# A fused attention and MLP-mixer kernel: rounding steps behind squares, pools in another order, sums and transposes at other places, last stores split

## The chip, the cores and the metric

The kernel runs on one core of a Trainium2 chip. The metric is the device time of one execution in microseconds (us), the median of several runs. A core has a matrix engine (TensorE, PE in the profile), a vector engine (VectorE, DVE), a scalar engine (ScalarE, ACT), GpSimd (POOL), and SyncE (SP), which here only issues DMAs. Each engine runs its own list of instructions in order, and waits where it needs what another one makes.

## The reference

Attention without a softmax, normalised by row and head, and then an MLP mixer over tokens and over channels. With B = 8, H = 8 heads, S = 576 tokens, D = 64 (512 channels):

```python
kv = einsum('bhsd,bhse->bhde', k, v)
o = einsum('bhsd,bhde->bhse', q, kv)
x = o / sqrt(mean(o * o, -1) + 1e-6) * g_norm            # then to (B, S, 512)
h = maximum(x.T @ w_tok1, 0) @ w_tok2                    # 576 -> 256 -> 576, over tokens
u = x + h.T
out = u + maximum(u @ w_ch1, 0) @ w_ch2                  # 512 -> 1536 -> 512, over channels
```

q, k and v are 32-bit floats. The four weights are 64-bit floats, which the kernel rounds to 32 bits itself; all matmuls are in 32 bits.

## The kernel before

**Attention and token mixing** work on pairs of batch elements, four pairs. For each pair, `kv` steps make the products of k and v, `a0` to `a4` make the attention outputs (`a4` is the remainder of 64 tokens of both elements), and for each of them `q` (square, on ACT), `g` (times `g_norm`, on DVE), `t` (sum of squares, on DVE), `m`, `r` and `i` (mean, root, inverse) and `s`, `d` or `p` (scaling on ACT, DVE or POOL) follow. `h..` and `hr` are the first token matmul, `u0` to `u8` the second; `z` copies an x tile into PSUM ahead of `u` as its start (a seed). The attention outputs of `a` stand in two PSUM buffers (`ps_o`, or `ps_r` for the remainder), so the tile after `a4` starts when the squares and gains of `a4` have read theirs. u is stored to DRAM by POOL's queue, and read back later.

The x tiles of even pairs come from the pool `xp0`, of odd pairs from `xp1`. The pools on the left side of SBUF lie in the order in which they are made, and the pools of the next stage take their room from the bottom when they are closed: first the three sums of `w_ch1` that `mix_ch1` makes (`late["w2"]`, 18,432 bytes a partition, as much as `xp0`), then the transposed u of the rest unit, then working buffers.

**The order of the work** is written out by hand: `play` reads lists of names, `start`, `middle`, `steady[0]`, `steady[1]` and `last`, one after the other. `middle` does the attention of pair 1 beside the token mixing of pair 0, and so on. A digit in them takes that many steps from the stream of rounding: for each of 14 blocks of the channel weights `scale` (two ACT instructions of 768 or 1024 elements a partition, which wait for the raw weights), `clamp`, `shift` and `add` (DVE). The scaling of the next block comes in one step with the shift of the one before. `lq0` loads q (transposed, `qT`) for the next pair, `l..` loads k and v, `f..` the raw weights, `x..` transposes u in blocks; all these DMAs are issued by SP, in one queue. As `a4` ends the use of one of the two `qT` buffers, `lq0` stands behind it.

**The rest unit.** Channel mixing has nine units of 512 tokens: eight of one batch element each, and one of the eight remainders of 64. The rest unit goes first and alone (`channel1_once`, `channel2_once`).

**Channel mixing** of the other units goes in four stages `g` of two units each, 1 to 4. Both matmuls use a scheme of seven products in place of eight, twice nested: an outer product `o` of sums of blocks of u (`outer_u`) and of the weights, and in it seven inner products (`inner_u`, places by `PLACE`) in three PSUM names, `ps_a`, `ps_b` (one buffer each) and `ps_d` (two). `put` files steps under a place; a place is one inner product on PE, about 1.30 us, and the steps follow it. `channel1` begins at place `b`; its outer product number i starts at `b + 7i`, and reads `ps_a` out at `b + 7i + 4` in its `second` (with a base, by a DVE addition, else by an ACT copy). The matmul at `b + 7i + 7` writes `ps_a` again. `add(3, 3, 1)` adds v1 to v3 in two halves, `turn_blocks` transposes u for the next stage from `xt`, four times with the DVE for each unit, and `put_blocks` stores every second result; `fetch_t` loads `xt`, of which there are two buffers.

**The end.** In the last outer product of the last stage the results go onto `xg` (u, read back), together with the sums of other outer products (`xadd`). `store_part` stores two of the four row tiles of the last batch element, `store_rest` the columns 256 to 511 of all remainders.

## Time and profile before

| | us |
|---|---|
| median of 3 runs | 805.42 (805.23 to 805.69) |
| the profiled execution, its own time | 807.61 |
| its span, first to last instruction | 805.80 |
| PE busy | 778.9 (97%) |
| DVE busy | 613.1 (76%) |
| ACT busy | 265.8 (33%) |
| POOL busy | 78.3 (10%) |
| mean DMA rate | 237 GB/s over the span |

Stages by the profile: attention and token mixing to about 203 us, the rest unit to 275.6, and then four stages of some 131 us. The profile has, for each instruction, when it started and how long it took, and for idle time ahead of it which engine or DMA ended that; in a timeline the columns are the start and the duration in us, the engine (with q: its queue, which issues), the line, the operation, its tiles, and in brackets the idle time before it. A table of waits has the total, the number and the longest. For stages it has the busy time of each engine and, last in the row, the clock granted to PE (1.00 is full), the busy share of the DMA engines and GB/s. PE's idle time matters most, since PE is busy nearly throughout; the issue of a DMA and its landing are apart by the time in the queue.

### The profile page before, as it was taken

The page shows a single profiled execution, that of the slowest core. Times are in us where ns is not written, and L with a number is a line of the kernel's source. Part 1 is how long each engine was busy: PE and PEld are TensorE (multiplying, and loading weights), DVE is VectorE, ACT ScalarE, POOL GpSimd, SP SyncE. Part 2 cuts the span into 40 slices and gives each one's busy share as a digit, 9 for nine tenths or more (in the row PEclk, how much of TensorE's full clock was granted, in tenths as well). Part 3 has the DMA queues.
Part 4 walks back from the last instruction along what each step waited for, and adds up shares of the span by engine and source line. Part 5 has one row for each costly group of instructions (what it writes and reads, how often), then busy time and mean ns, then how long its engine had stood idle before and what let it go on. Part 6 is the DMA issues. An engine that isn't in the chain of part 4 may idle for free.

```text
span 805.8 us, 14820 instructions
## 1 busy us (share of the span) xinstructions
PE 778.9 (97%) x5832; PEld 654.2 (81%) x5832; DVE 613.1 (76%) x906; ACT 265.8 (33%) x513; POOL 78.3 (10%) x91
## 2 busy tenths in 40 slices
PE   6999989999999999999999999999999999999996
PEld 5655545543888888899988899998889998889996
DVE  2667867679666877988867889877798875788975
ACT  2356454655120123521133251122352113325210
POOL 1211111021530000001100001010000110000101
PEclk9999989999999999999999999999999999999999
DMA  9999999676689795598997579889559889555864
GB/s 294 311 344 328 364 309 381 227 267 227 222 285 318 274 334 166 155 282 215 252 235 222 156 207 272 249 195 285 141 154 298 200 230 231 169 156 145 206 151 79
DMA packets 128117, 192.11 MB, mean 238 GB/s; under 512 B 9392, under 2 KB 87728, under 8 KB 128048
## 3 DMA queue, kind: packets, MB, share of 16 engines
q1 hardware_dynamic: 111760, 167.67, 66.2%
q0 software_dynamic: 14656, 22.02, 13.4%
q10 hardware_dynamic: 1632, 1.47, 0.6%
q8 instruction: 46, 0.75, 0.4%
q14 instruction: 23, 0.19, 0.1%
HBM read 138.31 MB, written 52.82 MB: 237 GB/s over the span
## 4 chain that ended last, share of the span: by engine, by line
PE 73%; DVE 2%; issue 1%; ACT 0%; DVEq 0%
PE ps_d L132 27%; PE ps_a L132 18%; PE ps_b L132 18%; PE ps_v L132 5%; PE ps_c L132 3%; PE ps_w L132 2%; PE ps_u L132 1%; DVE us L123 1%; DVE v L123 0%; DVE u L123 0%; DVE ui L123 0%; DVE w_ch L173 0%; DVE w_ch L168 0%; ACT ps_u L129 0%; DVE xg L123 0%
## 5 line engine op out<-in xcount | busy, mean ns | idle before, releaser
L132 PE MATMUL ps_d<-ui,w 128*128 128x256 f32 x504 | 118.6, 379 | 0.0
L132 PEld LDWEIGHTS ps_d<-ui,w 128*128 128x128 f32 x504 | 95.2, 190 | 12.7
L123 DVE TENSOR_TENSOR v<-v,v 128x1536 f32<-128x1536 f32 (+2 forms) x70 | 103.5, 1484 | 0.3
L129 ACT COPY ps_d<-ps_a 128x768 f32<-128x768 f32 (+1 forms) x56 | 32.0, 571 | 210.2 <-PE ps_a L132 210.2
L132 PE MATMUL ps_b<-w,sv 128*128 128x128 f32 x672 | 84.6, 276 | 0.0
L132 PE MATMUL ps_a<-w,v 128*128 128x128 f32 x672 | 84.2, 275 | 0.0
L132 PEld LDWEIGHTS ps_a<-w,v 128*128 128x128 f32 x672 | 79.9, 192 | 0.2
L132 PEld LDWEIGHTS ps_b<-w,sv 128*128 128x128 f32 x672 | 79.5, 192 | 0.2
L132 PE MATMUL ps_u<-h,w_tok 128*128 128x512 f32 (+1 forms) x160 | 69.5, 621 | 1.8 <-ACT ps_u L129 1.5
L132 PE MATMUL ps_d<-w,v 128*128 128x128 f32 x528 | 66.2, 275 | 0.0
L132 PE MATMUL ps_h<-x,w_tok 128*128 128x512 f32 (+1 forms) x160 | 65.5, 603 | 0.1
L126 ACT ACTIVATE v<-v 128x768 f32<-128x768 f32 (+1 forms) x54 | 42.6, 821 | 66.2 <-DVE v L123 60.6
L132 PEld LDWEIGHTS ps_d<-w,v 128*128 128x128 f32 x528 | 62.7, 192 | 0.2
L132 PE MATMUL ps_d<-w,sv 128*128 128x128 f32 x480 | 60.1, 275 | 0.0
L132 PEld LDWEIGHTS ps_d<-w,sv 128*128 128x128 f32 x480 | 57.1, 192 | 0.2
L132 PEld LDWEIGHTS ps_u<-h,w_tok 128*128 128x128 f32 (+1 forms) x160 | 25.5, 184 | 34.2 <-issue 26.7
L132 PEld LDWEIGHTS ps_h<-x,w_tok 128*128 128x128 f32 (+1 forms) x160 | 26.1, 189 | 32.1 <-issue 28.2
L132 PE MATMUL ps_a<-uT,w 128*128 128x256 f32 x192 | 47.1, 381 | 4.9 <-DVE v L123 4.9
L1116 POOL DMA_DIRECT2D out_dram<-us x11 | 14.1, 1278 | 386.7 <-ACT us L129 345.6
L132 PEld LDWEIGHTS ps_a<-uT,w 128*128 128x128 f32 x192 | 35.9, 190 | 11.1 <-DVE v L123 6.5
L439 DVE TENSOR_TENSOR x<-ps_o,g_sb 128x512 f32<-128x512 f32 x32 | 21.5, 687 | 29.9 <-PE ps_o L132 25.1
L123 DVE TENSOR_TENSOR v<-ps_b,u 128x768 f32<-128x768 f32 x28 | 26.7, 954 | 22.5 <-PE ps_b L132 22.0
(145 smaller groups left out, 1233.4 us busy)
## 6 DMA issues: line engine op xcount, KB each, us to landing
w<-parts SPq DMA_DIRECT2D x168, 384.0 KB, 3.9
w<-parts SPq DMA_DIRECT2D x56, 192.0 KB, 3.3
qT<-in_q_dram SPq DMA_DIRECT2D x8, 1152.0 KB, 9.9
uT<-blocks SPq DMA_DIRECT2D x36, 256.0 KB, 5.5
k_in<-in_k_dram SPq DMA_DIRECT2D x16, 512.0 KB, 9.0
out_dram<-x POOLq DMA_DIRECT2D x16, 512.0 KB, 5.9
v_in<-in_v_dram SPq DMA_DIRECT2D x14, 512.0 KB, 9.7
raw<-in_moe_w_ch_dram SPq DMA_DIRECT2D x8, 768.0 KB, 9.6
```

Source lines behind the costliest of these rows:

```text
L123: keep(engine.tensor_tensor(out=o, in0=a, in1=b, op=op))
L126: keep(nc.scalar.activation(o, a, AF.Relu))
L129: keep(nc.scalar.copy(o, a))
L132: keep(nc.tensor.matmul(*a, **kw))
L439: keep(nc.vector.tensor_mul(x, bank[c, h], g_sb.to_broadcast([P, number(c), D])))
L1116: keep(nc.gpsimd.dma_start(to.rearrange("t p e -> p t e"), a, accum_op=ALU.add))
```

## The change

- `xp0` is made after `inp` (k, v, g), `qtp` (q) and `work`, so that it lies above them.
- In `middle` a rounding step moves from the row of `u5` to the end of the row of `a4`; in `steady[0]` one moves from the row of `u4` to the same place. Both are steps with a scaling.
- In `channel1` the two halves of `add(3, 3, 1)` move from places 17 and 22 to 21 and 24, the first four `turn_blocks` (with their `put_blocks` and `fetch_t`) from 5, 8, 11 and 14 to 3, 6, 9 and 12, and the fourth subtraction of `outer_u` from 17 to 25.
- At the end the second half's `xadd` of product 5 moves from 47 to 44 and the first half's from 45 to 46. `store_rest` moves from 48 to 45. The last element's second half is stored in two pieces: columns 384 to 511 from ACT's queue at 48, and columns 256 to 383 from SP's at 49.

```diff
-    xps = [pool("xp0", 4, "left", left), pool("xp1", 4, "right", right)]
+    xp1 = pool("xp1", 4, "right", right)
     inp = pool("inp", 1, "left", left)
     qtp = pool("qtp", 2, "left", left)
     work = pool("work", 1, "left", left)
+    xps = [pool("xp0", 4, "left", left), xp1]
...
-        for place, step in zip((17, 22), add(3, 3, 1)):
+        for place, step in zip((21, 24), add(3, 3, 1)):
...
-        for k, place in enumerate((5, 8, 11, 14, 50, 52, 67, 77)):
+        for k, place in enumerate((3, 6, 9, 12, 50, 52, 67, 77)):
...
-        for place, step in zip((-2, 1, -1, 17), outer_u(g)):
+        for place, step in zip((-2, 1, -1, 25), outer_u(g)):
...
-            for place, steps in ((38, [xadd(0, 6)]), (41, [xadd(1, 7)]), (45, [xadd(0, 5)]),
-                                 (47, [xadd(1, 5)]),
-                                 (48, [do(store_part, 0, 2), do(store_rest)]), (49, [do(store_part, 2, 4)])):
+            for place, steps in ((38, [xadd(0, 6)]), (41, [xadd(1, 7)]), (44, [xadd(1, 5)]),
+                                 (45, [store_rest]), (46, [xadd(0, 5)]),
+                                 (48, [do(store_part, nc.scalar, 2, 4, P, DH), do(store_part, nc.sync, 0, 2, 0, DH)]),
+                                 (49, [do(store_part, nc.sync, 2, 4, 0, P)])):
...
-    def store_part(lo, hi):
-        dma(out[B - 1, lo * P:hi * P, DH:].rearrange("(t p) e -> p t e", p=P), xg[NG - 1][:, lo:hi])
+    def store_part(queue, lo, hi, a, z):
+        dma(out[B - 1, lo * P:hi * P, DH + a:DH + z].rearrange("(t p) e -> p t e", p=P),
+            xg[NG - 1][:, lo:hi, a:z], queue)
...
-        "u4 z6 f1", "a2 q20 g21 q21 g20 s10", "u5 t20 t21 1 f2", "a4 q40 g41 q41 g40 lq0", "u6 t40 t41 1 l10",
+        "u4 z6 f1", "a2 q20 g21 q21 g20 s10", "u5 t20 t21 f2", "a4 q40 g41 q41 g40 lq0 1", "u6 t40 t41 1 l10",
...
-        "u4 z6 1 l11", "a4 q40 g41 q41 g40 lq0", "u5 d11 t40 t41 1", "a3 q30 g31 q31 g30 lq1",
+        "u4 z6 l11", "a4 q40 g41 q41 g40 lq0 1", "u5 d11 t40 t41 1", "a3 q30 g31 q31 g30 lq1",
```

## The prediction

> **What bounds the kernel now.** First the page's head and the table of who waited for whom, TensorE alone.

> ```profile
> span 805.8 us, 14820 instructions
> PE 778.9 (97%) x5832; PEld 654.2 (81%) x5832; DVE 613.1 (76%) x906; ACT 265.8 (33%) x513; POOL 78.3 (10%) x91
> PE ps_kv L132 <- DMA v_in<-in_v_dram: 7.1, 2, 6.4
> PE ps_a L132 <- DVE v L123: 4.9, 4, 1.2
> PE ps_o L132 <- ACT sq L443: 4.9, 3, 3.3
> PE ps_u L132 <- ACT ps_u L129: 1.5, 1, 1.5
> ```

> TensorE is the bound: it is idle 26.9 us, of which 6.4 are the first load and 7.2 come after its last matmul. No change to busy DVE or ACT time pays as such; only a removed wait of PE, or a shorter end, does. So each wait was looked up in the timelines. The largest:

> ```profile
> 111.60 1.98 PE L132 MATMUL ps_u<-h,w_tok 128*128 128x512 f32 x4
> 116.89 2.17 PE L132 MATMUL ps_o<-kvp,qT 64*64 64x64 f32 x64 [3.31 <-ACT sq L443]
> 114.64 0.89 ACT L158 ACTIVATE w_ch<-raw 128x768 f32<-128x768 f32 x1 [1.77 <-DMA raw<-in_moe_w_ch_dram]
> 116.19 0.65 ACT L443 ACTIVATE sq<-ps_r 128x256 f32<-128x256 f32 x2
> 118.00:120.00 2.00, 2.00 (x40) 1.37 (x36) 2.00 (x5) 0.60 (x1) 0.72 (x1) 0.50 1.13 374
> ```

> The remainder tile `a4` ended at 111.7, but its squares started at 116.19: ahead of them on ACT stood a scaling of rounding that waited for its weights until 114.64. The next attention tile needs the same PSUM buffers, so PE stood 3.31 us, and then ran at half clock (the last line is a stage: its third number from the end is the granted clock, 0.50). From the start of that tile to the next `ps_kv` took 126.41 - 116.89 = 9.52 us; the same instructions a pair later took 169.32 - 162.55 = 6.77. The slow clock thus cost 2.75 us more. The like wait in `middle` (72.42) is 1.03 us with no loss of clock.

> The other three places:

> ```profile
> 182.23 1.76 DVE L123 TENSOR_TENSOR w<-w_ch 128x1536 f32<-128x1536 f32 x1 [5.10 <-DMA out_dram<-x]
> 191.09 1.17 ACT L158 ACTIVATE w_ch<-raw 128x1024 f32<-128x1024 f32 x1 [3.25 <-DVE w_ch L173]
> 193.84 9.00 PE L132 MATMUL ps_u<-h,w_tok 128*128 128x512 f32 x24 [1.53 <-ACT ps_u L129]
> 429.66 1.75 DVE L123 TENSOR_TENSOR v<-v,v 128x1536 f32<-128x1536 f32 x1
> 431.33 1.22 DVE L123 TENSOR_TENSOR us<-uT,us 128x1024 f32<-128x1024 f32 x1
> 432.46 0.95 DVE L123 TENSOR_TENSOR v<-ps_a,v 128x768 f32<-128x768 f32 x1
> 433.47 1.56 PE L132 MATMUL ps_a<-uT,w 128*128 128x256 f32 x6 [1.23 <-DVE v L123]
> 798.48 2.45 SPq L120 DMA_DIRECT2D out_dram<-xg  x3
> 798.68 0.42 DVE L123 TENSOR_TENSOR xg<-ps_d,xg 128x256 f32<-128x256 f32 x1 [0.23 <-PE ps_d L132]
> ```

> At 182 the sums of `w_ch1` wait for stores out of the x tiles whose room they take; DVE, then ACT's scaling, then a seed copy, then PE are late in turn. At 429 a 1.75 us sum and a 1.22 us subtraction stand ahead of the read of `ps_a` that PE's place 21 needs. At the end three stores queue on SP.

> [...] half clock came 2.7 us into the 3.31 us wait and stayed 6.8 us; the 1.53 us wait did nothing. [...] those engines are over 95% busy from 104 to 140 us.

> **Part 1, scalings behind the squares** (rows `a4` of `middle` and `steady[0]`). No instruction is added. The squares then run at 111.8 to 112.5, after the seed copy `z6`, and the a3 tile follows `u5` at once. At its face this is worth 1.03 + 3.31 + 2.75 = 7.1 us. What is late next: the scaling still waits to 114.6, ends at 116.3, and the a3 squares and DVE's `add` of the rounding stand behind it (DVE to about 117). So a3's statistics come only 3.35 us earlier than 124.9. They feed `x` tiles that PE needs only after `a0` of the next pair, so they are hidden. But that `a0` needs a transfer:

> ```profile
> qT<-in_q_dram SPq DMA_DIRECT2D x1, 1152.0 KB, 10.3
> 135.91 1.16 PE L132 MATMUL ps_o<-kvp,qT 64*64 64x64 f32 x64
> ```

> It is issued at 121.04 and lands at 131.3 (10.3 later) in a full queue; `a0` came at 135.91, so 4.6 us of slack stood behind it. PE would now come at 135.91 - 7.1 = 128.8 (the steps one by one, with 0.1 for a3's buffers: 129.0). Nor can qT come earlier: its issue is held by the queue, not by a buffer, with at most 0.5 us of idle DMA (100 to 108, shares 0.92 and 0.96) to use. Rather later: the stores of this pair's last u tiles (issued 126.75 to 130.04; 1.05 MB, 2.6 us of all DMA engines by the per-queue shares) move up by some 3.4 us and interleave ahead of it. Before, 0.3 us of them lay ahead of 131.3. Bounds for the landing: 130.8 (only the idle DMA time used) to 133.6 (all stores ahead). I take 132.5. PE then waits 3.5 us and resumes 3.4 us earlier than before. Such a wait (3.31) halved the clock before[...]. I take yes, two chances in three, at the same 2.75. Part 1 nets -3.4 + 2.75 = **-0.65 us** (-3.4 with full clock).

> **Part 2, even x tiles above the inputs.** The sums now take the room of k, v and g, last read at 149.7 (kv) and 166.5 (gains), in place of that of tiles stored until 181.9. DVE starts them at 177.1 and all behind moves 5.1 us forward: rounding's add ends about 186, ACT's scaling goes straight after the seed copies (187.8), the seed is in place before 192.3. **-1.53 us**. Where the stall goes: nowhere near; later work of `last` is PE's own. If the sums waited elsewhere, the cost is the 1.53 kept.

> **Part 3, channel mixing, places 3 to 25** (four stages). The sum's halves go from 17 and 22 to 21 and 24, the subtraction from 17 to 25. DVE reads `ps_a` at 429.75 in place of 432.46, done before PE's place 21 at 432.25. -1.23 each. What is late next: the sum (1.75) at 24 and the subtraction (1.22) at 25 end at 441.3, so the read of `ps_b` at 26 ends at 442.2, and PE writes `ps_b` at 442.6: 0.4 us left. The transposes (0.7 us each) at 3, 6, 9, 12 fit DVE's idle 1.95 us before 412.93 and the gap before 418.04. Each brings its DMAs along SP's queue: four of blocks, one fetch of xt. They pass one 384 KB weight fetch, which lands about 3 us later than 421.47; it is used at 429.5: hidden. In the first stage xt is late: the fourth transpose waited until 295.46 for a transfer of 7.0 us. Now it stands before a read of `ps_d` (place 13), which PE needs at 294.98. One weight fetch fewer ahead brings it in at 293 to 294.5; with 0.7 for the transpose and 0.9 for the read PE stalls 0 to 1.1; I take 0.4. Sum: -4.9 + 0.4 = **-4.5 us** (-4.9 to -3.8).

> **Part 4, the end.** `store_rest` goes at 45, after `xadd(1, 5)` (ready 793.5): its two issues and 0.5 MB are out of the way by 798. `xadd(0, 5)` goes behind the `ps_a` read, where DVE has room. Before, the last store was issued at 799.69, though its data were there at 799.1, and took 5.1 us to 804.83 behind 0.77 MB. The first of the three, with the DMA engines free, took 2.35 us. Now SP has one store ahead (issued about 797.8) and the last, of 128 KB, goes at 799.15; with 2.35 it lands at 801.5. **-3.3 us** (-2.8 to -3.5).[...]

> Sum: -0.65 - 1.53 - 4.5 - 3.3 = -10.0 on the span of 805.8 (that execution's time was 807.61, 1.8 around it, unchanged). The median is 805.42, so 795.4.

> **Rivals.** (a) qT and the wait as said[...]: 792.7.[...] (b) qT is no bound, because the queue runs ahead of PE more than I allow: 7.1 instead of 0.65: 789.0. Against: the DMA engines' 95%. (c) The moved transposes wait for xt in three stages (the last has none) and hold `ps_d` 1.1 to 1.5 us each, 4.1 in all where I took 0.4: 795.4 + 3.7 = 799.1. Against: in stages two and three xt landed at 423.38 and 552.88, and should now land at some 422 and 552, before the read ahead of it ends (422.95, 553.7). (d) Slower: qT's transfer slips behind others. The other parts give 9.3, so `a0` has to start after 135.91 + 9.3 - 2.75 = 142.5, 11 us later than qT lands now; that is about 4 MB more ahead of it at 375 GB/s, where the stores bring 1.05. It would take a changed order on SP. (The last raw weights were issued at 172.28, after fetches that the text has later, so that order isn't wholly the text's.)

> **Chances.** Forecast 0.45, (a) 0.22, (b) 0.15, (c) 0.10, no change 0.03, (d) 0.05. Faster by over 0.2% (what a measurement of this kernel can about tell from no change) 0.92, within 0.03, slower 0.05. Forecast's own range 793.8 to 797.0 (the qT and tail bounds); with (a), (b) and most of (c) 788.5 to 799.0.

> **What would show it.** No wait of PE on `sq` near 113; a new one before `a0` near 129 to 132 with qT's landing at its end, and half clock behind it; DVE's sums without the 5.1; no wait of `ps_a` on DVE, perhaps a short one of `ps_d` in the first stage; the last store landing 2.4 us after the last add. The forecast is wrong if qT lands before PE comes, or if DVE's waits at 9 and 12 reach PE in each stage.

## The result, and the profile after

The changed kernel takes 795.81 us (median of 4 runs, 794.60 to 796.61); the kernel before took 805.56 beside it (4 runs, 805.23 to 806.31). The ratio is 0.9876, with an interval of 0.9859 to 0.9894: 9.75 us, or 1.2%, faster, where 795.4 us had been predicted. The profiled execution took 795.84 us, 1.8 of it around its span. In the kernel after, the helpers' lines are one higher: matmuls are L133, DVE's additions L124, the squares L444.

First the head of the page after (busy time of each engine), and then its table of TensorE's waits (what waited for what, the total, how often, the longest).

```profile
span 794.1 us, 14832 instructions
...
PE 777.8 (98%) x5832; PEld 655.1 (83%) x5832; DVE 612.8 (77%) x906; ACT 265.7 (33%) x513; POOL 78.3 (10%) x91
```

```profile
PE ps_kv L133 <- DMA v_in<-in_v_dram: 7.0, 2, 6.2
PE ps_o L133 <- DMA qT<-in_q_dram: 4.8, 1, 4.8
PE ps_o L133 <- ACT sq L444: 0.8, 2, 0.5
PE ps_r L133 <- ACT sq L444: 0.2, 1, 0.2
```

PE's busy time is within 1.1 us of before, so only waits and the end have changed. The rows of `ps_a` on DVE (4.9) and of `ps_u` on ACT (1.5) are gone. The row of `ps_o` on the squares has fallen from 4.9 to 0.8, and a wait of 4.8 for q has come in its place.

Attention of the third pair and the start of the fourth, in PE's timeline after, and in the stages (busy time of PE, PEld, DVE, ACT and POOL; then the granted clock, the DMA share, GB/s):

```profile
112.42 1.34 PE L133 MATMUL ps_o<-kvp,qT 64*64 64x64 f32 x64
113.69 5.57 PE L133 MATMUL ps_u<-h,w_tok 128*128 128x512 f32 x16
119.09 2.50 PE L133 MATMUL ps_kv<-v_in,k_in 128*64 128x64 f32 x80
121.52 7.13 PE L133 MATMUL ps_h<-x,w_tok 128*128 128x512 f32 x16
133.41 1.99 PE L133 MATMUL ps_o<-kvp,qT 64*64 64x64 f32 x64 [4.76 <-DMA qT<-in_q_dram]
135.33 10.55 PE L133 MATMUL ps_h<-x,w_tok 128*128 128x512 f32 x24
145.81 1.16 PE L133 MATMUL ps_o<-kvp,qT 64*64 64x64 f32 x64
```

```profile
134.00:136.00 2.00, 2.00 (x55) 1.71 (x49) 0.52 (x1) 0.50 (x1) 0.00 (x0) 0.50 1.05 386
```

The tile behind the remainder starts at 112.42 without a wait (before: 116.89, after 3.31). PE is then at `a0` of the last pair at 128.6, and stands 4.76 us until q is there. The clock falls to half during this wait, at 131.56, and `a1` starts at 145.81, where it started at 145.98 before. By then all of part 1 but 0.17 us has been given back.

DVE's timeline after, with the sums of `w_ch1` and two additions in the second stage of channel mixing; and PE's, with place 21 of that stage:

```profile
176.28 0.68 DVE L165 TENSOR_SCALAR w_ch<-w_ch 128x1024 f32<-128x1024 f32 x1
176.88 1.75 DVE L124 TENSOR_TENSOR w<-w_ch 128x1536 f32<-128x1536 f32 x1
...
426.22 0.96 DVE L124 TENSOR_TENSOR v<-ps_a,v 128x768 f32<-128x768 f32 x1
...
430.02 1.75 DVE L124 TENSOR_TENSOR v<-v,v 128x1536 f32<-128x1536 f32 x1
```

```profile
428.61 1.46 PE L133 MATMUL ps_a<-uT,w 128*128 128x256 f32 x6
```

The sums begin at 176.88 with no idle time ahead of them (before: 182.23, after 5.10). The read of `ps_a` ends at 427.18, before PE comes to write it at 428.61; the long sum now follows at 430.02.

The end: in DVE's timeline the last addition, and then the issues of the last stores (how many, KB each, and the median time from issue to landing).

```profile
790.87 0.42 DVE L124 TENSOR_TENSOR xg<-ps_d,xg 128x256 f32<-128x256 f32 x1 [1.13 <-PE ps_d L133]
```

```profile
out_dram<-xg SPq DMA_DIRECT2D x2, 256.0 KB, 2.8
...
out_dram<-xg ACTq DMA_DIRECT2D x1, 128.0 KB, 2.0
out_dram<-xg SPq DMA_DIRECT2D x1, 128.0 KB, 1.8
```

The last piece lands 1.8 us after its issue, where the store that ended the kernel before took 5.1.

Offsets of the same matmul in the two traces give the account of this pair of executions (us, after less before):

| at | before | after | offset | step |
|---|---|---|---|---|
| `ps_r`, the remainder tile, pair 3 | 110.97 | 109.88 | -1.09 | most of it the wait in `middle`, 1.03 before and 0.24 after |
| tile behind it | 116.89 | 112.42 | -4.47 | -3.38: wait for the squares gone |
| next `ps_kv` | 126.41 | 119.09 | -7.32 | -2.85: half clock gone |
| `a0` of pair 4 | 135.91 | 133.41 | -2.50 | +4.82: wait for q |
| `a1` of pair 4 | 145.98 | 145.81 | -0.17 | +2.33: half clock |
| seeded tile of `last` | 193.84 | 191.97 | -1.87 | -1.70: sums of `w_ch1` |
| first matmul of channel mixing | 275.39 | 273.42 | -1.97 | -0.10 |
| end of the last matmul | 798.64 | 790.83 | -7.81 | -5.97 over four stages, +0.13 |
| last landing | 804.83 | 793.15 | -11.68 | -3.87: tail |
| span | 805.8 | 794.1 | -11.7 | |

The medians differ by 9.75 alone, 2 us less: the profiled execution of the kernel before (807.61) was itself some 2 us above its median (805.56).

### The profile page after: what moved, and what is told of

It reads as the page before. It is cut to its first block, busy times and chain, and to the rows that moved or that the text cites. A ratio compares the mean times of both kernels' runs of the same rounds, so it can differ in the third digit from the quotient of the medians.

```text
span 794.1 us, 14832 instructions
## 1 busy us (share of the span) xinstructions
PE 777.8 (98%) x5832; PEld 655.1 (83%) x5832; DVE 612.8 (77%) x906; ACT 265.7 (33%) x513; POOL 78.3 (10%) x91
## 4 chain that ended last, share of the span: by engine, by line
PE 94%; DMA 2%; DVE 1%; ACT 1%; issue 0%; ACTq 0%
PE ps_d L133 28%; PE ps_b L133 19%; PE ps_a L133 19%; PE ps_u L133 8%; PE ps_h L133 7%; PE ps_v L133 5%; PE ps_c L133 3%; PE ps_kv L133 2%; PE ps_o L133 2%; PE ps_w L133 2%; DMA qT<-in_q_dram 2%; PE ps_j L133 1%; ACT x L494 1%; DMA v_in<-in_v_dram 1%; DVE x L440 0%; DVE ms L461 0%
## 5 line engine op out<-in xcount | busy, mean ns | idle before, releaser
L133 PE MATMUL ps_d<-ui,w 128*128 128x256 f32 x504 | 118.6, 379 | 0.0
L133 PEld LDWEIGHTS ps_d<-ui,w 128*128 128x128 f32 x504 | 95.2, 190 | 12.7
L124 DVE TENSOR_TENSOR v<-v,v 128x1536 f32<-128x1536 f32 (+2 forms) x70 | 103.5, 1483 | 0.3
L133 PE MATMUL ps_b<-w,sv 128*128 128x128 f32 x672 | 84.6, 276 | 0.0
L133 PE MATMUL ps_a<-w,v 128*128 128x128 f32 x672 | 84.2, 275 | 0.0
L133 PEld LDWEIGHTS ps_a<-w,v 128*128 128x128 f32 x672 | 79.8, 192 | 0.2
L133 PEld LDWEIGHTS ps_b<-w,sv 128*128 128x128 f32 x672 | 79.5, 192 | 0.2
L133 PE MATMUL ps_u<-h,w_tok 128*128 128x512 f32 (+1 forms) x160 | 67.2, 606 | 0.2
L133 PE MATMUL ps_h<-x,w_tok 128*128 128x512 f32 (+1 forms) x160 | 67.0, 613 | 0.1
L133 PE MATMUL ps_d<-w,v 128*128 128x128 f32 x528 | 66.2, 275 | 0.0
L133 PEld LDWEIGHTS ps_d<-w,v 128*128 128x128 f32 x528 | 62.7, 192 | 0.3
L133 PE MATMUL ps_d<-w,sv 128*128 128x128 f32 x480 | 60.1, 275 | 0.0
L133 PEld LDWEIGHTS ps_d<-w,sv 128*128 128x128 f32 x480 | 57.1, 192 | 0.2
L133 PEld LDWEIGHTS ps_h<-x,w_tok 128*128 128x128 f32 (+1 forms) x160 | 26.7, 193 | 33.0 <-issue 29.9
L133 PEld LDWEIGHTS ps_u<-h,w_tok 128*128 128x128 f32 (+1 forms) x160 | 24.8, 179 | 31.0 <-issue 25.9
L133 PE MATMUL ps_a<-uT,w 128*128 128x256 f32 x192 | 46.7, 379 | 0.0
L133 PE MATMUL ps_b<-ui,w 128*128 128x256 f32 x168 | 40.8, 379 | 0.0
L133 PEld LDWEIGHTS ps_a<-uT,w 128*128 128x128 f32 x192 | 36.2, 190 | 4.8
## 6 DMA issues: line engine op xcount, KB each, us to landing
qT<-in_q_dram SPq DMA_DIRECT2D x8, 1152.0 KB, 10.0
```

Of the source, the lines that this page charges most:

```text
L124: keep(engine.tensor_tensor(out=o, in0=a, in1=b, op=op))
L133: keep(nc.tensor.matmul(*a, **kw))
```

## The experiments

Each is the kernel after with one edit, but for e7 and e12, which start from e6, and e13, which starts from the kernel before. The edits show only the words of a row that change. The kernel before ran on the same chips: 805.92 us with e1 to e4, 805.78 with e6 to e9, 805.18 with e10 to e13. e4 and e10 can't be told from the kernel after by their ratios, and serve as its stand-ins on the first and the third chip (795.0 and 795.79).

**e1: part 1 undone.**

```diff
-"u5 t20 t21 f2", "a4 q40 g41 q41 g40 lq0 1"       # middle
+"u5 t20 t21 1 f2", "a4 q40 g41 q41 g40 lq0"
-"u4 z6 l11", "a4 q40 g41 q41 g40 lq0 1"           # steady[0]
+"u4 z6 1 l11", "a4 q40 g41 q41 g40 lq0"
```

> The changed kernel with part 1 alone undone: both rounding steps stand again ahead of the squares of the remainder tile. Theory A (the wait for qT took the place of the wait for the squares, and the half clock came again): PE stands 3.3 us at the tile after the remainder and not at all ahead of the next pair's first tile; the time is within 0.3 us of the changed kernel, 795.8 to 796.1 if before is 805.6. Theory B (part 1 pays its 7 us and another part lost its gain): 802 to 803.

Measured: 793.72 us (792.90 to 794.87), ratio 0.9841 [0.9823, 0.9859]: 1.3 us under the stand-in on its chip, 2.1 under the kernel after. Its PE timeline, the tile behind the remainder, `a0` and `a1`:

```profile
116.42 1.34 PE L133 MATMUL ps_o<-kvp,qT 64*64 64x64 f32 x64 [2.57 <-ACT sq L444]
...
133.12 1.16 PE L133 MATMUL ps_o<-kvp,qT 64*64 64x64 f32 x64 [0.47 <-DMA qT<-in_q_dram]
...
143.20 1.16 PE L133 MATMUL ps_o<-kvp,qT 64*64 64x64 f32 x64
```

With the old order PE waits 2.57 for the squares, and then another 0.47 for q: `a0` starts at 133.12, no later than after the change (133.41). q's landing sets this point in either order. Behind these shorter waits the clock stays full in this trace (granted 1.00 from 116 to 144; 0.997 to 1.000 over the runs, against 0.995 to 0.998 after the change), and so `a1` comes at 143.20 in place of 145.81. The large value of part 1 is refuted. The medians make it a cost of 1.3 to 2.1 us beside the other parts, but the runs of e1 overlap with those of the stand-in (793.00 to 796.35), so that this run alone does not tell a small cost from none. The cost lies in the clock: e4's trace, which differs from this one in nothing but part 1 up to channel mixing and has full clock too (0.999), gets there at 270.55, this one at 270.80.

**e2: part 2 undone.**

```diff
-    xp1 = pool("xp1", 4, "right", right)
+    xps = [pool("xp0", 4, "left", left), pool("xp1", 4, "right", right)]
...
-    xps = [pool("xp0", 4, "left", left), xp1]
```

> The changed kernel with the pools in the old order. Theory A: DVE's sums of w_ch1 wait some 5 us for stores again, PE stands at the seed copy again, and the time is 1.7 us above the changed kernel (797.5 if before is 805.6). Rival: the later start of DVE's work is made up for by the slack of the next stages, 0 to 0.3 us.

Measured: 796.87 us (796.21 to 798.07), 0.9881 [0.9863, 0.9899]; 1.9 over the stand-in on its chip. In its table of waits (lines count as in the kernel before) the one on the seed is back at its old size:

```profile
PE ps_u L132 <- ACT ps_u L129: 1.6, 1, 1.6
```

So is its cause, 5.15 us of DVE waiting for stores of x ahead of the sums at 182.38. Part 2 works as predicted.

**e3: the sums and the subtraction of part 3 back; the transposes stay.**

```diff
-        for place, step in zip((21, 24), add(3, 3, 1)):
+        for place, step in zip((17, 22), add(3, 3, 1)):
...
-        for place, step in zip((-2, 1, -1, 25), outer_u(g)):
+        for place, step in zip((-2, 1, -1, 17), outer_u(g)):
```

> The changed kernel with the sum of v at places 17 and 22 and the subtraction at 17 again, the transposes left at their new places. Theory A: PE waits for DVE's read of ps_a in all four stages[...], 6.0 us in all (801.8 if before is 805.6). Rival (the transposes' move is what freed DVE): 0 to 1.5 us.

Measured: 801.75 us (800.74 to 803.54), 0.9941 [0.9925, 0.9956]; 5.9 over the kernel after, 6.7 over the stand-in. In its table of waits the old row is back; after it PE's timeline around the second of the four:

```profile
PE ps_a L133 <- DVE v L124: 4.9, 4, 1.2
```

```profile
428.67 1.46 PE L133 MATMUL ps_d<-ui,w 128*128 128x256 f32 x6
431.36 1.56 PE L133 MATMUL ps_a<-uT,w 128*128 128x256 f32 x6 [1.22 <-DVE v L124]
432.75 1.46 PE L133 MATMUL ps_b<-ui,w 128*128 128x256 f32 x6
```

The idle time shown is 1.22, but starts of products lie 1.295 apart where nothing waits. Here they lie 2.69 and 1.39 apart: 1.39 + 0.10 = 1.49 us are lost. Four times 1.49 is 5.96, and the offset over the four stages of the two kernels is 5.97. The wait thus costs a fifth more here than its idle time.

**e4: the transposes of part 3 back.**

```diff
-        for k, place in enumerate((3, 6, 9, 12, 50, 52, 67, 77)):
+        for k, place in enumerate((5, 8, 11, 14, 50, 52, 67, 77)):
```

> The changed kernel with the four transposes at places 5, 8, 11 and 14 again, the sums left at their new places. Theory A: nothing, within 0.3 us of the changed kernel, since DVE has idle time at both. Rival (they must be out of the way of the reads at 12 to 18): PE waits in stages 1 to 3, 0.5 to 1.5 us each, 1.5 to 4.5 us in all.

Measured: 795.0 us (793.00 to 796.35), 0.9857 [0.9839, 0.9876]. From the first matmul of channel mixing to the end of the last its trace has 517.41 us, and that of the kernel after has 517.41 too (e3: 523.84). In these two traces moving the transposes brings nothing and costs nothing.

**e6: q's load ahead of two loads of k and v, in `steady[0]`.** If q's landing is what takes part 1's gain, an earlier q must give it back.

```diff
-        "u0 i0 1", "u1 1 d00 l10", ...
-        "u4 z6 l11", "a4 q40 g41 q41 g40 lq0 1", ...
+        "u0 i0 1", "u1 1 d00", ...
+        "u4 z6", "a4 q40 g41 q41 g40 lq0 l10 l11 1", ...
```

> The changed kernel with the load of q for the last pair issued ahead of that pair's two later loads of k and v, not behind them. Theory A (that load alone held PE ahead of the next pair's first tile): it lands near 127, PE does not wait there, the clock stays full, and the profiled span falls by the wait and the half clock, 4.8 + 2.3 us, to about 787; the time is 788.7 (up to 790 if the scaling that waits for raw weights near 139 now holds the relus). Theory C (another transfer or engine is just behind): 792 or more.

Measured: 790.08 us (789.07 to 790.76), 0.9802 [0.9787, 0.9818]: 5.7 under the kernel after, and just past the upper end of what was expected. Its PE timeline at `a0` and `a1` of the last pair:

```profile
129.15 1.16 PE L133 MATMUL ps_o<-kvp,qT 64*64 64x64 f32 x64
130.25 9.05 PE L133 MATMUL ps_h<-x,w_tok 128*128 128x512 f32 x24
139.23 1.16 PE L133 MATMUL ps_o<-kvp,qT 64*64 64x64 f32 x64
```

q is issued at 111.18 and lands at 124.24; it took 13.1 us, more than the 12.1 in the kernel after (121.15 to 133.27), so it is the place in SP's queue that helps, not a faster transfer. `a0` follows the `ps_h` without a wait, and the clock is full in all runs (0.999 to 1.000). 6.6 us are gained at `a1` (139.23 against 145.81), of which a new wait of 0.7 at 151.93 takes some back (e12).

**e7: e6 with part 1 undone.**

```diff
-"u5 t20 t21 f2", "a4 q40 g41 q41 g40 lq0 1"            # middle
+"u5 t20 t21 1 f2", "a4 q40 g41 q41 g40 lq0"
-"u4 z6", "a4 q40 g41 q41 g40 lq0 l10 l11 1"            # steady[0]
+"u4 z6 1", "a4 q40 g41 q41 g40 lq0 l10 l11"
```

> As the run before it, but both rounding steps ahead of the squares again. Theory A: with q there in time part 1 pays what its waits cost, 1.1 us and 2.6 to 3.4 us without half clock, up to 2.9 more with it, so this is 3.7 to 7.4 us slower than the run before it. Theory C: no difference over 0.5 us.

Measured: 794.25 us (792.65 to 796.18), 0.9856 [0.9837, 0.9874]: 4.2 slower than e6. In its table of waits the squares are back:

```profile
PE ps_o L133 <- ACT sq L444: 3.6, 3, 2.0
```

In its trace the wait at the tile behind the remainder is 2.00 us, and half clock follows for 3.41. The same edit that brings nothing in the kernel after is worth 4.2 where q is there in time. That settles part 1: what it removes is real, and the next wait on the path took it. The reverse holds too. Without part 1 an early q brings nothing: e7 (0.9856) is no faster than e1 (0.9841), where q is late. Each of the two edits pays only with the other.

**e9 and e11: PE kept busy while it waits for q.** Thirty, or sixteen, matmuls of an identity go ahead of `a0` in the last pair; their results are not used. They tell the price of the half clock from that of the wait.

```diff
-    def keep_warm(n):
+    def keep_warm(n, name="h"):
...
-        o = ps["h"].tile([P, DM], F32, name="ps_j", tag="h")
+        o = ps[name].tile([P, DM], F32, name="ps_j", tag=name)
...
+    more["j30"] = do(keep_warm, 30, "o")      # e11: j16, 16
...
-        "h01 1 f9", "a0 q00 ...
+        "h01 1 f9", "j30 a0 q00 ...
```

> The changed kernel with 30 idle-time matmuls of 128x128[...] ahead of the first tile of the last pair, where PE waits for q. Theory A (the wait's second cost is the half clock, about 2.3 us[...]): PE reaches the tile before q lands, the clock stays full in each run, the profiled span is 791.7 and the median 793.5. Rival (the slow stretch behind the wait has another cause): 795.8, half clock as before.

> As the run with 30 warming matmuls, but with 16 of them (3.6 us of PE by the rate of that run, 0.112 us for each of two passes), so that they end before q lands. Theory A: the clock stays full in each run and the first tile of the last pair starts when q lands, near 133.5: the profiled span is 791.7 and the median 793.6, some 2 us under the changed kernel. Rival (the half clock costs nothing in the end): 795.8.

Measured: e9 795.92 us (795.60 to 796.11), 0.9875 [0.9860, 0.9890]; e11 793.51 (792.94 to 794.50), 0.9855 [0.9839, 0.9871]. PE's timelines, e9 first, then e11:

```profile
129.12 6.86 PE L133 MATMUL ps_j<-ident 128*128 128x128 f32 x60
135.91 1.28 PE L133 MATMUL ps_o<-kvp,qT 64*64 64x64 f32 x64
```

```profile
128.69 3.73 PE L133 MATMUL ps_j<-ident 128*128 128x128 f32 x32
133.40 1.16 PE L133 MATMUL ps_o<-kvp,qT 64*64 64x64 f32 x64 [0.98 <-DMA qT<-in_q_dram]
```

e9's expectation fell with the author's estimate of the time of thirty matmuls, about half of the 6.86 us that they took: each shows as two of 0.114 us, so they ran to 135.91, 2.1 us past q's landing (133.79), and ate what the full clock gave. With sixteen PE is free again when q lands; the clock stayed at 0.999 or above in every run, and 2.3 us are gained on the same-chip stand-in (795.79), as the offsets had it. So q's wait in the trace of the kernel after costs 4.8 us itself and 2.3 by the clock.

**e8: the end undone.**

```diff
-    (44, [xadd(1, 5)]), (45, [store_rest]), (46, [xadd(0, 5)]),
-    (48, [do(store_part, nc.scalar, 2, 4, P, DH), do(store_part, nc.sync, 0, 2, 0, DH)]),
-    (49, [do(store_part, nc.sync, 2, 4, 0, P)])
+    (45, [xadd(0, 5)]), (47, [xadd(1, 5)]),
+    (48, [do(store_part, nc.sync, 0, 2, 0, DH), do(store_rest)]),
+    (49, [do(store_part, nc.sync, 2, 4, 0, DH)])
```

> The changed kernel with the end as it was (sums, rest store and last store). Theory A: from PE's last matmul to the last landing 6.2 us in place of 2.3, so 3.9 us above the changed kernel, 799.7. Rival (the earlier stores only moved the traffic): under 1.5 us.

Measured: 798.32 us (797.24 to 801.05), 0.9907 [0.9889, 0.9925]; 2.5 over the kernel after, where 3.9 was expected. In its trace the last landing comes 5.75 us after the last matmul, 3.4 more than after the change (2.32). The runs scatter by 3.8 us, and the medians can't be brought closer to the trace than that. The same trace shows, in the first stage of channel mixing, the risk of the moved transposes: here PE's row of waits, and then DVE's on `xt`.

```profile
PE ps_d L133 <- DVE v L124: 1.1, 1, 1.1
```

```profile
DVE y L612 <- DMA xt<-out_dram: 4.7, 2, 2.4
```

In the kernel after DVE waited 3.1 in those two places, and PE not at all. The second transpose was 1.5 us later there, and the reading of `ps_d` behind it held PE. So the moved transposes are neutral in most of the traces, and cost 1.1 in this one and 0.2 in e3's.

**e10: the last half stored whole, 256 KB from SP.**

```diff
-    (48, [do(store_part, nc.scalar, 2, 4, P, DH), do(store_part, nc.sync, 0, 2, 0, DH)]),
-    (49, [do(store_part, nc.sync, 2, 4, 0, P)])
+    (48, [do(store_part, nc.sync, 0, 2, 0, DH)]),
+    (49, [do(store_part, nc.sync, 2, 4, 0, DH)])
```

> The changed kernel with the last element's second half stored whole, 256 KB from SP as the last issue; the rest's stores stay early. Theory A (of the 3.9 us at the end, nearly all comes from the stores taken out of the queue; the split saves the time of 128 KB): 0.3 to 0.5 us above the changed kernel, from the last addition to the last landing 2.2 us in place of 1.9. Rival (the split is what pays): 1.5 us or more.

Measured: 795.79 us (794.62 to 796.61), 0.9881 [0.9864, 0.9897], the same as the kernel after. Its row of issues at the end, the last store among them:

```profile
out_dram<-xg SPq DMA_DIRECT2D x3, 256.0 KB, 2.2
```

From the last matmul to the last landing its trace has 2.69 us, against 2.32 with the split. What part 4 gains comes from `store_rest` and `xadd` moved out of the way; splitting the store brings 0.4 in the trace, too little to tell in the medians.

**e12: e6, with one rounding step of the last pair moved behind the relus.** The remaining wait of e6 came from relus of `h11` that stood on ACT behind a scaling waiting until 139.34 for its weights.

```diff
-        "h10 t00 t01 1 x21", "h11 1", "hr 1 z2 f10", ...
+        "h10 t00 t01 1 x21", "h11", "hr 1 z2 1 f10", ...
```

> As the run with q ahead of both loads, with one more rounding step moved: the scaling that waits for raw weights until 139 goes behind the relus of the first token matmul. Theory A: PE's last wait of 0.7 us before the second token matmul goes, and with it 0.7 to 0.9 us: 789.2 against 790.1. Rival: another wait takes its place, 790.1.

Measured: 789.19 us (789.03 to 789.51), 0.9801 [0.9787, 0.9816]: 6.6 under e10 on the same chip, 16 under the kernel before. Two rows of its waits:

```profile
PE ps_o L133 <- ACT sq L444: 0.9, 3, 0.5
...
PE ps_u L133 <- ACT ps_u L130: 0.2, 1, 0.2
```

The wait on the seed has fallen from 0.7 to 0.2. By the ratios e12 can't be told from e6 (0.9801 and 0.9802); by the medians, on two chips, it is 0.9 less. Either one beats both kernels.

**e13: the kernel before with part 1 alone.**

```diff
-"u5 t20 t21 1 f2", "a4 q40 g41 q41 g40 lq0"        # middle
+"u5 t20 t21 f2", "a4 q40 g41 q41 g40 lq0 1"
-"u4 z6 1 l11", "a4 q40 g41 q41 g40 lq0"            # steady[0]
+"u4 z6 l11", "a4 q40 g41 q41 g40 lq0 1"
```

> The kernel before with part 1 alone. Theory A (the end of the wait is set by q either way, and one long wait halves the clock more often than two short ones): PE's wait for the squares goes, one of 3.4 to 5.4 us for q comes, and the time is not below the kernel before: 0 to 2 us above it. Theory B (part 1 pays when it stands alone): 799 to 802.

Measured: 807.28 us (14 runs, 804.01 to 808.71) against 805.18 (19 runs, 804.16 to 809.34): 2.1 us by the medians, 0 to 2.1 by the ratio, 1.0013 [1.0000, 1.0026]. Two rows of its waits:

```profile
PE ps_o L132 <- DMA qT<-in_q_dram: 3.5, 1, 3.5
...
PE ps_o L132 <- ACT sq L443: 0.8, 2, 0.5
```

With the other parts out, the same exchange of one wait for another. The runs' mean granted clocks show its price: 8 of these 14 runs have 0.993, and 1 of the 19 of the kernel before on that chip is as low. The fastest run of each, at 0.998 and 0.999, are alike (804.01 and 804.16). This mean also holds the half clock behind the last matmul, which costs nothing (1.9 us of it in e13's trace, 3.4 in that of the kernel before).

## Why the prediction was right, and where it was not

The total was right (795.4 against 795.81), in part by luck: its steps missed in both directions, and the misses nearly cancelled.

**Part 1** was predicted at -0.65 net (forecast) from a face value of 7.1. Its mechanism was right for the wait: q, issued by SP at the same place as before (121.15), becomes the bound; it landed at 133.27, inside the bounds of 130.8 to 133.6 but 0.8 behind the 132.5 taken; PE came at 128.65, not 129.0, waited 4.8 and not 3.5, and ran at half clock after it. That it would was the author's estimate, two chances in three, from the one wait of 3.31 in the trace of before. That POOL's stores share the DMA engines with q, which their busy share of 95% from 104 to 140 us alone does not show, is to be seen in the transfers of the kernel before from 121 to 132 us: the queue of SP's loads took 85.5% of the time of the 16 engines, POOL's 18.3%. The term that failed is the 2.75 of half clock *removed*. It was read from one execution of the kernel before and credited in full, but it does not belong to each execution of that kernel: its best runs, at a granted clock of 0.998 or 0.999, take 804.2 to 804.7, and e1, which has the old order, waits 2.57 with the clock full. Without the half clock ahead of it, q's own landing is the fixed point in both orders (132.99 in e1, 133.27 after), and the wait removed at 112 is simply waited at 129. The landing at 131.3 in the trace of before, on which the 4.6 us of slack stood, belongs to that one execution as well. Two waits of 2.6 and 0.5 thus become one of 3.1 to 5.4, and the long one slows the clock more often, as e13's clocks show (0.993 in 8 of 14 runs, as low in 1 of 19 without part 1); of the seven traces that have it (after, e2, e3, e4, e8, e10, e13), all but e4's (0.999) have a mean clock of 0.995 to 0.997. The sign was wrong: a gain of 0.65 lies outside e13's interval, 0 to 2 us slower, and e1 points the same way.

**Part 2**, -1.53: met. The offset is -1.70, and e2's medians give -1.1 to -1.9.

**Part 3**, -4.5: right in mechanism, too small in size, at -5.97 in the traces and -5.9 to -6.7 in e3. Of the 1.47 missing, 1.07 is the term "-1.23 each", which is 1.49; 0.4 is the allowance for a late `xt`, which did not come in the trace after, and came as 1.1 in e8's and 0.2 in e3's. Rival (c), transposes that hold PE in three stages, did not come true: the table after has no wait of `ps_d`, and without the move (e4) channel mixing takes as long.

**Part 4**, -3.3: -3.87 in the trace and -2.5 in e8's medians. The term that was off is the 2.35 from the last issue to its landing, taken from a store of 256 KB; the 128 KB took 1.8. The split on two queues had no part worth telling (e10).

**The basis.** The sum of -10.0 was made on a span of 805.8 and then taken off a median that stood 2.2 below that execution's own time. The half clock was thus credited against a median that holds only part of it. What part 1 was too favourable by, about 2 us, was balanced by the 1.5 and up to 0.6 that parts 3 and 4 were too small by. Of the rivals, (a), the same wait for q with full clock behind it, at 792.7, has its size confirmed by e11 (2.3 for 2.75) but not its case; (b), q no bound, at 789.0, is what e6 and e12 bring about by an edit (790.08, 789.19), but its price of 7.1 for part 1 was too high: with q there in time part 1 is worth 4.2 (e7), and the rest comes from parts 3 and 4; (d) did not happen.

Behind which of these waits the clock fell to half can be read from the traces. Their length alone doesn't decide it: waits of 2.57 (e1) and 3.39 (e4) left the clock full; 2.00 (e7), 3.05 (e10) and 3.54 (e13) brought 3.41 us of half clock; 3.31 (before) and 4.76 (after) brought 6.83. But in the traces of before and after the times at which the profile's records of the granted clock begin lie whole multiples of 3.413 us apart (before: 10.47, 116.28, 123.11 and 802.36, steps of 31, 2 and 199; after: 12.10, 131.56, 138.39 and 793.75, steps of 35, 2 and 192), so a trace can be cut into stretches of that length. Here are those about the wait in before, after, e4, e10 and e7 (length, PE's busy time, its instructions, granted clock, DMA share, GB/s):

```profile
112.87:116.28 3.41, 0.71 (x2) 1.00 0.99 338
116.28:119.70 3.42, 2.81 (x65) 0.50 1.06 379
119.70:123.11 3.41, 3.41 (x5) 0.50 1.06 362
...
128.15:131.56 3.41, 0.50 (x2) 1.00 1.03 411
131.56:134.98 3.42, 1.57 (x60) 0.50 1.05 396
134.98:138.39 3.41, 3.41 (x20) 0.50 1.06 384
...
127.84:131.25 3.41, 1.65 (x4) 1.00 1.03 413
131.25:134.67 3.42, 1.80 (x66) 1.00 1.04 399
...
129.82:133.24 3.42, 0.90 (x61) 1.00 1.03 405
133.24:136.65 3.41, 3.41 (x23) 0.50 1.06 386
...
113.25:116.66 3.41, 1.41 (x51) 1.00 1.00 380
116.66:120.07 3.41, 3.41 (x34) 0.50 1.02 406
```

e4's wait of 3.39 us lay across two stretches, and each still had 1.65 us or more of matmuls. The waits of before, after, e10 and e7 left 0.71, 0.50, 0.90 and 1.41 in one, and half clock followed at its end. In before and after the next stretch, at half clock, had 2.81 and 1.57, and another at half clock followed; that one was full (3.41), and full clock came behind it. One stretch of e1 had 1.41 as well, and its clock stayed full. So half clock went with how much of one stretch a wait emptied rather than with the wait's length, and where the borders fall differs from run to run (131.25 in e4, 131.56 in after, 133.24 in e10). A limit can't be read from so few, and no run here moved the borders.

## What to carry to other kernels

Before a removed wait is credited, find what the waiting engine needs next and when that lands; here a transfer issued from a full queue landed as its place in the queue had it (133.27 behind two loads, 124.24 ahead of them), and moving it made 5.7 us of a reordering that alone had brought nothing. Take the clock's share out of a single trace before adding it to a sum against a median: see from several runs' granted clocks whether it belongs to the kernel, and leave out what lies behind the last matmul. And where the engine must wait all the same, cheap matmuls in the gap can keep its clock if they are sized to end before the data land: here sixteen (3.73 us) kept it at 0.999 or above and brought 2.3 us (e11), and thirty (6.86 us), which ended 2.1 us past the landing, brought nothing (e9).
